# Scores of the first ten heads as one plain float32 product, and the SoLU layer beside head ten

## The chip, the cores and the metric

The kernel runs on one core of one Trainium2 chip. The metric is the device time of one execution in microseconds. TensorE is called PE in the profile, VectorE DVE, ScalarE ACT, GpSimd POOL, SyncE SP.

## The reference

Three layers are computed one after the other.

```python
# attention: 4 batches, 8 heads, 576 tokens, head size 64
scores = scale * q @ k.T
cum    = cumsum(log(clip(f, 1e-4, 1)))
scores = where(causal, -1e9, scores + cum[:, None] - cum[None, :])
attn   = softmax(scores) @ v
# SoLU layer: 2304 tokens, 512 -> 1024 -> 512
h   = x @ w_in
ln  = layernorm(h * softmax(h)) * g_ln
x   = ln @ w_out
# mixture of 8 experts, the best 2 of each token, 512 -> 1024 -> 512
logits = x @ w_gate + log1p(exp(x @ w_noise)) * noise
out    = sum over the top 2 of weight * relu(x @ w1[e]) @ w2[e]
```

All data are float32, and so is the result.

## The kernel before

**Number formats on PE.** A float32 operand is mostly split into a rounded float32r part and the float32r remainder, and a product is made of float32r products of these parts. The product of attention weights with V is plain float32 in the first `PLAIN_AV` = 13 heads, and split after them.

**One head.** Thirty-two heads are worked off in order; heads 2p and 2p+1 form a pair. `load_raw` brings queries and keys of a head, both transposed, as one tile of 128 partitions by 576. `prep` (L216) makes four operand tiles of it: QA and KB by copies on ScalarE (L223, L224), KA and QB by copies on GpSimd (L225, L226), the remainders by a subtraction on VectorE (L227, into KB) and one on GpSimd (L228, into QB). Four sets of these tiles exist, so a head uses set h % 4. Two more rows in the upper half of KA hold the head's decay (the cumulated logarithm, in two parts), and the same rows of QA hold ones, so that the decay is added by the product itself. `load_ext` loads these rows. `set_init` fills what is not loaded with zeros and ones.

`scores` (L248) computes five row blocks of 128 queries, up to the diagonal; the last block of 64 rows is shared by the two heads of a pair. Each block takes two products, QB with KB (L283) and QA with KA (L284). VectorE subtracts the mask and takes the row maximum (L286), ScalarE takes the exponential and the row sum (L288). `normalize` scales the rows on GpSimd (L301). `etrans` transposes the blocks on PE (L321), ScalarE copies them out (L325); from head 13 on VectorE also makes a remainder. `av` multiplies with V (L350 plain, L370 split) and ScalarE writes the result to XT (L354). Accumulators are three large ones (last row block, transposes, product with V) and two small ones (the other row blocks).

**Front.** `cum_prep` computes the decay of all heads on 32 partitions: clip on VectorE (L179), logarithm on ScalarE (L180), scan on VectorE (L184), two parts (L186, L187), and writes it to memory. Then heads 0 to 12 run alone. Beside each of them one or two of sixteen chunks of the SoLU weights are unpacked and split (`load_w`, L393, by `FRONT_W`): ACT, DVE four times, ACT, then GpSimd (L412) or DVE (L417), all through a single tile `wasm`.

**Middle.** After head 12, `init_dram` (L680) writes zeros to the output (18 DMAs) and fills two tables, from tiles that share buffers with the weight chunks. Then `merge` interleaves the text of the remaining heads with SoLU tiles of 128 tokens: `m_split` (L431, L432) on GpSimd, two times twelve products (L444), statistics, eight transposes (L488), 24 products (L499), gate and routing. The four batches give groups of heads 13 to 17 with tiles 0 to 3, heads 18 to 25 with tiles 4 to 8, heads 26 to 33 with tiles 9 to 12. The remaining tiles and the experts follow without attention.

**Order.** The text order is only a priority: a planner of the framework places the instructions of each engine, and each engine then works its list off in order. So the products of tile 0 (L444) run from 151 us on, beside head 12.

Of the kernel before, what the change touches and what calls it, by code (L numbers as in the profile page):

```python
# [9 lines left out]
F32 = mybir.dt.float32  # L10
F32R = mybir.dt.float32r
# [4 lines left out]
ALU = mybir.AluOpType  # L16
AX = mybir.AxisListType

MASKED = 1.0e9

PLAIN_AV = 13

TOP_OF_SMALLEST = struct.unpack("f", struct.pack("I", 896 << 20))[0]

# [2 lines left out]
def kernel(  # L27
# [18 lines left out]
    nc = tc.nc  # L46
    P = 128
# [29 lines left out]
    att = ExitStack()  # L77
    ap_ = att.enter_context(tc.tile_pool(name="att", bufs=1, side="right"))

    wpools = [wp, wp]  # L80
    turn = [0]

# [13 lines left out]
    def f32(t):  # L96
        return t.bitcast(F32)


    identf = cst.tile([P, P], F32, name="identf")  # L100
    make_identity(nc, identf)

    swapf = cst.tile([P, P], F32, name="swapf")
    for j in range(2):
        nc.vector.tensor_copy(swapf[:, j * D:(j + 1) * D], identf[:, (1 - j) * D:(2 - j) * D])

    maskr = cst.tile([P, FULL], BF, name="maskr")
    nc.vector.memset(maskr, 0.0)
    nc.gpsimd.affine_select(out=maskr[:, FULL - P:], in_=maskr[:, FULL - P:], pattern=[[-1, P]], base=0,
                            channel_multiplier=1, compare_op=ALU.is_ge, fill=-MASKED / QSC)  # L110
    maskt = cst.tile([P, S], BF, name="maskt")
    nc.vector.memset(maskt, 0.0)
    for j in range(2):
        nc.vector.tensor_copy(maskt[j * TAIL:(j + 1) * TAIL, FULL:],
                              maskr[j * TAIL:(j + 1) * TAIL, FULL - P + j * TAIL:FULL - P + (j + 1) * TAIL])
    SUMS = [cst.tile([P, NQ], F32, name=f"sums{i}") for i in range(3)]
    for t in SUMS:
        nc.vector.memset(t, 1.0)
# [4 lines left out]
    count = cst.tile([P, E], F32, name="count")  # L123
    ebase = cst.tile([P, E], F32, name="ebase")
    mhalf = cst.tile([P, 1], F32, name="mhalf")

    def routing_constants():
        nc.vector.memset(ones_b, 1.0)
# [20 lines left out]

    UP, EXT = slice(0, D), slice(D, P)  # L150
    SETS = 4
    QW = FULL + P
    QA, QB, KA, KB = ([ap_.tile([P, n], F32R, name=f"{nm}{i}") for i in range(SETS)]
                      for nm, n in (("qa", QW), ("qb", QW), ("ka", S), ("kb", S)))
# [4 lines left out]
    def set_init(i, eng):  # L159
        j = i % 2  # L160
        eng.memset(f32(KA[i])[EXT], 0.0)
        eng.memset(f32(QA[i])[EXT], 0.0)
        eng.memset(f32(QA[i])[D:D + 2, HELD[j]], 1.0)
        eng.memset(f32(QA[i])[UP, FREE[j]], 0.0)
        eng.memset(f32(QB[i])[:, FREE[j]], 0.0)

    set_init(0, nc.gpsimd)
    set_init(1, nc.vector)

    VN = [ap_.tile([P, NQ, P], F32, name=f"vn{i}") for i in range(2)]  # L170
    for t in VN:
        nc.vector.memset(t[:D, NQ - 1, :], 0.0)
    CC = []

    def cum_prep():
# [16 lines left out]

    def load_raw(h):

        if h < NH:
            RAW[h] = ap_.tile([P, S], F32, tag="raw", name=f"raw{h}", bufs=2)
            nc.sync.dma_start(RAW[h], qk[h])

    def load_ext(h):

        if h < NH:
            i = h % SETS
            if h < 2:
                for j in range(2):
                    nc.sync.dma_start(f32(KA[i])[D + j:D + j + 1, :], f32(CC[0])[h:h + 1, j, :])
            else:
                nc.sync.dma_start(f32(KA[i])[D:D + 2, :], cumd[h])

    def load_v(p):
        if p < NH // 2:  # L210
# [4 lines left out]

    def prep(h):  # L216

        if h >= NH:
            return
        i = h % SETS  # L220
        raw = RAW.pop(h)
        d = HELD[h % 2]
        nc.scalar.activation(QA[i][UP, d], raw[UP], AF.Copy)  # L223
        nc.scalar.activation(KB[i][EXT], raw[EXT], AF.Copy)  # L224
        nc.gpsimd.tensor_scalar(KA[i][UP], f32(KB[i])[EXT], 1.0, 1.0, op0=ALU.mult, op1=ALU.mult)  # L225
        nc.gpsimd.tensor_scalar(QB[i][UP, d], f32(QA[i])[UP, d], 1.0, 1.0, op0=ALU.mult, op1=ALU.mult)  # L226
# [4 lines left out]
    VS2 = []  # L231

    def vs_init():
        VS2.extend(vsp.tile([P, NQ, P], F32R, name=f"vs{i}") for i in range(2))

    def vsplit(h):
# [11 lines left out]
    def scores(h, rs):  # L248
# [11 lines left out]
        for r in rs:  # L260
# [17 lines left out]
            for a, z in cuts:  # L278
                o = ps[:, o0 + a:o0 + z]
                for j in heads:  # L280
                    i = (h // 2 * 2 + j) % SETS
                    qs = LAST[j] if tail else slice(j * P + diag, j * P + diag + P)
                    nc.tensor.matmul(o, QB[i][:, qs], KB[i][:, a:z], start=j == heads[0], stop=False)  # L283
                    nc.tensor.matmul(o, QA[i][:, qs], KA[i][:, a:z], start=False, stop=j == heads[-1])  # L284
            e = ap_.tile([P, N], F32, tag=f"e{r}", name=f"e{h}_{r}", bufs=2)
# [47 lines left out]
    def av(h):  # L333
# [38 lines left out]
        lo = vsp.tile([P, S], F32, tag="avl", name=f"avl{h}", bufs=1)[r0:r0 + D]  # L372
        nc.scalar.activation(lo, ps[D:, o0:o0 + S], AF.Copy)
        x = XT[b][r0:r0 + D, hh // 2, :]
        nc.vector.tensor_add(x, ps[:D, o0:o0 + S], lo)
# [314 lines left out]
            nc.sync.dma_start(ov[c], zt)  # L690

    def attn_stream(h):
        load_raw(h + 3)
        load_ext(h + 2)
        if h < NH:
            scores(h, (4, 3))
            yield 1200
            scores(h, (2, 1, 0))
            yield 940
            normalize(h)  # L700
        for _ in range(FRONT_W[h] if h < len(FRONT_W) else 0):
            more_w()
        prep(h + 2)
        if 0 <= h - 2 < NH:
            av(h - 2)
            yield 1700
        if h % 2 == 1:
            load_v(h // 2 + 1)
        vsplit(h)
        if 0 <= h - 1 < NH:  # L710
            etrans(h - 1, 0)
            yield 1000
            etrans(h - 1, 1)
            yield 600
# [35 lines left out]
    def run_all(g_):  # L750
        for _ in g_:
            pass
# [23 lines left out]
    def more_w():  # L776
        if wn[0] < 2 * KC + FC:
            load_w(wn[0])
            wn[0] += 1
# [2 lines left out]
    stage = stack.enter_context(tc.tile_pool(name="stage", bufs=1, side="right"))  # L782
    cum_prep()
    for h in range(2):
        load_raw(h)
    load_v(0)
    for h in range(2):
        prep(h)
        load_ext(h)
    load_raw(2)  # L790
    for i in (2, 3):
        set_init(i, nc.gpsimd)
    load_small()
    routing_constants()

    def att_part(hs):
        for h in hs:
            yield from attn_stream(h)


    FRONT_W = (1, 1, 1, 1, 1, 1, 1, 1, 1, 2, 2, 2, 1)
    run_all(att_part(range(len(FRONT_W))))
    init_dram()
    stack.close()
    vsp = att.enter_context(tc.tile_pool(name="vsp", bufs=1, side="right"))
# [151 lines left out]
```

## Time and profile before

| | |
|---|---|
| median of 3 runs | 1045.58 us (1044.43 to 1046.62) |
| profiled execution | 1044.73 us, of which the span of the profile is 1043.0 us |
| PE busy | 939.2 us, 90% of the span |
| VectorE, ScalarE, GpSimd busy | 561.0, 444.5, 469.0 us |
| mean granted clock of PE | 0.963 of full speed |

The time of the profiled execution is its span plus 1.73 us. Busy times of different engines overlap. Idle time of an engine is put down to the instruction whose end released it.

### The profile page before, as it was taken

To read this page: it belongs to the slowest core of one execution; us is meant where nothing else is said; L and a number is where in the kernel's file an instruction comes from. 1 tells how busy PE (TensorE), PEld (TensorE's weight loads), DVE (VectorE), ACT (ScalarE), POOL (GpSimd) and SP (SyncE) were. 2 spreads that over 40 slices of the span, in tenths; PEclk is the share of its full clock that TensorE was granted. 3 is DMA by queue.
4 is the path that set the end of the run, shared out by engine and by line. 5 is a ranking of instruction groups with operands and counts; after the bars stand their busy time and mean duration, and the time that the engine had idled before them with its cause. 6 is when DMAs were issued, how large, how long until landed. Compare 5 with 4: busy or idle time off the path is not lost. (4 is left out here: it accounts for less than half of the span.)

```text
span 1043.0 us, 14547 instructions
## 1 busy us (share of the span) xinstructions
PE 939.2 (90%) x5164; PEld 809.4 (78%) x5164; DVE 561.0 (54%) x1387; ACT 444.5 (43%) x831; POOL 469.0 (45%) x561
## 2 busy tenths in 40 slices
PE   3767787999999889999978999999999999999995
PEld 2545565787888778877867789898998989898994
DVE  7665877577778667756556244444443334444220
ACT  4676775556666555543343033232231323232110
POOL 7786776667767755543432223231413232230201
PEclk9988888999999999999988999999999999999998
DMA  5223336111111100031034335453434344451201
GB/s 142 85 78 107 96 107 220 63 45 35 49 42 45 46 11 22 11 92 51 23 92 112 93 117 189 141 165 122 141 112 147 102 156 149 141 168 61 78 11 38
DMA packets 55221, 96.54 MB, mean 93 GB/s; under 512 B 15398, under 2 KB 24870, under 8 KB 55144
## 3 DMA queue, kind: packets, MB, share of 16 engines
q1 hardware_dynamic: 44792, 66.41, 21.1%
q0 software_dynamic: 10352, 29.15, 8.4%
q8 instruction: 43, 0.70, 0.3%
q14 instruction: 34, 0.28, 0.1%
HBM read 76.16 MB, written 20.40 MB: 93 GB/s over the span
## 5 line engine op out<-in xcount | busy, mean ns | idle before, releaser
L649 PE MATMUL f<-fxh,we 128*128 128x256 f32 (+1 forms) x1024 | 172.3, 310 | 0.8 <-ACT fxh L632 0.8
L667 PE MATMUL f<-we,fhh 128*128 128x512 f32 x640 | 161.9, 396 | 0.0
L649 PEld LDWEIGHTS f<-fxh,we 128*128 128x128 f32 x1024 | 155.9, 189 | 1.2 <-ACT fxh L632 1.0
L667 PEld LDWEIGHTS f<-we,fhh 128*128 128x128 f32 x640 | 117.8, 188 | 24.4
L606 POOL DMA_INDIRECT row<-xdram,gi x40 | 40.2, 1005 | 211.2 <-PE fxT L629 197.3
L283 PE MATMUL s<-kb,qb 128*128 128x512 f32 (+3 forms) x192 | 73.6, 393 | 50.3 <-POOL qb L228 23.4
L654 DVE SCALAR_TENSOR_TENSOR fhl<-f,fhh 128x768 fp32r<-128x768 f32 (+1 forms) x64 | 52.7, 823 | 119.3 <-ACT fhh L653 110.8
L288 ACT ACTIVATE e<-e,nmax 128x384 f32<-128x384 f32 (+4 forms) x144 | 83.0, 577 | 60.6 <-DVE nmax L286 59.9
L301 POOL TENSOR_SCALAR e<-e,rc 128x256 f32<-128x256 f32 (+3 forms) x144 | 93.6, 667 | 31.9 <-DVE rc L298 14.3
L653 ACT ACTIVATE fhh<-f 128x768 fp32r<-128x768 f32 (+1 forms) x64 | 45.0, 704 | 139.8 <-PE f L649 129.8
L649 PE MATMUL f<-fxl,we 128*128 128x256 f32 (+1 forms) x512 | 96.3, 310 | 0.0
L283 PEld LDWEIGHTS s<-kb,qb 128*128 128x128 f32 x192 | 40.8, 214 | 70.3 <-POOL qb L228 26.8
L586 DVE TENSOR_TENSOR we<-raw,we 128x1024 fp32r<-128x1024 f32 x64 | 78.4, 1235 | 29.9 <-ACT we L585 26.8
L444 PE MATMUL m<-w_it,xh 128*128 128x512 f32 x288 | 85.2, 414 | 6.2 <-POOL xh L431 3.6
L585 ACT ACTIVATE we<-raw 128x1024 fp32r<-128x1024 f32 x64 | 66.9, 1056 | 53.5 <-PE f L667 24.7
L675 POOL DMA_INDIRECT out_dram<-y,gi x40 | 41.7, 1041 | 103.9 <-DVE y L674 79.4
L674 DVE SCALAR_TENSOR_TENSOR y<-f,tab,pv 128x512 f32<-128x512 f32 x35 | 26.3, 751 | 112.6 <-PE f L667 112.6
L667 PE MATMUL f<-we,fhl 128*128 128x512 f32 x320 | 80.4, 393 | 2.3 <-issue 2.3
L649 PEld LDWEIGHTS f<-fxl,we 128*128 128x128 f32 x512 | 80.7, 189 | 0.0
L632 ACT ACTIVATE fxh<-fxT 128x512 fp32r<-128x512 f32 x40 | 23.4, 596 | 129.5 <-PE fxT L629 129.5
L286 DVE CUSTOM_DVE_ANT_0 e<-s,maskr 128x512 f32<-128x512 f32 (+3 forms) x128 | 60.6, 485 | 32.8 <-PE s L284 26.5
L667 PEld LDWEIGHTS f<-we,fhl 128*128 128x128 f32 x320 | 60.0, 188 | 16.3 <-issue 2.7
(157 smaller groups left out, 1824.4 us busy)
## 6 DMA issues: line engine op xcount, KB each, us to landing
raw<-in_moe_w_dram SPq DMA_DIRECT2D x64, 512.0 KB
raw<-in_qk_dram SPq DMA_DIRECT2D x32, 288.0 KB
out_dram<-zt SPq DMA_DIRECT2D x18, 256.0 KB
xdram<-x SPq DMA_DIRECT2D x18, 256.0 KB
vn<-in_v_dram SPq DMA_DIRECT2D x16, 256.0 KB
wraw<-in_moe_w_in_dram SPq DMA_DIRECT2D x8, 512.0 KB
wraw<-in_moe_w_out_dram SPq DMA_DIRECT2D x8, 512.0 KB
row<-xdram,gi POOLq DMA_INDIRECT x40
```

The lines of the kernel that those rows point to most:

```text
L283: nc.tensor.matmul(o, QB[i][:, qs], KB[i][:, a:z], start=j == heads[0], stop=False)
L286: nc.vector.tensor_tensor_reduce(e, ps[:, o0:o0 + N], mask, -QSC, 3.0e38, ALU.add, ALU.min, nmax[:, r:r + 1])
L288: nc.scalar.activation(e, e, AF.Exp, bias=nmax[:, r:r + 1], scale=-1.0, accum_out=sums[:, r:r + 1])
L301: nc.gpsimd.tensor_scalar(e, e, rc[:, r:r + 1], 1.0, op0=ALU.mult, op1=ALU.mult)
L444: nc.tensor.matmul(ps, a[:, kk, :], w[:, kk, n * 512:(n + 1) * 512], start=i == 0, stop=i == 3 * KC - 1)
L585: nc.scalar.activation(hi[:, d], raw, AF.Copy)
L586: nc.vector.tensor_sub(lo[:, d], raw, f32(hi)[:, d])
L649: nc.tensor.matmul(ps[:, j], w[:, kk, (c + j) * P:(c + j + 1) * P], x[:, kk, :], start=i == 0, stop=i == 3 * KC - 1)
L653: nc.scalar.activation(hh[:, d], ps, AF.Relu)
L654: nc.vector.scalar_tensor_tensor(hl[:, d], ps, 0.0, f32(hh)[:, d], op0=ALU.max, op1=ALU.subtract)
L667: nc.tensor.matmul(ps, a[:, kk, d], w[:, kk, :], start=i == 0, stop=i == 3 * EC - 1)
L675: nc.gpsimd.indirect_dma_start(out[:, :], bass.IndirectOffsetOnAxis(ap=si[:, j:j + 1], axis=0), y, None, bounds_check=NTOK - 1, oob_is_err ...
```

## The change

For heads 0 to 9 (`PLAIN_S` = 10) queries and keys are loaded by two DMAs straight into operand tiles QP and KP, which also hold the decay rows and the ones; `prep` does nothing for them, and each row block takes one plain float32 product of QP and KP where it took two float32r ones. There are four sets of QP and KP, in a pool that is closed when head 10 begins. The split tiles are made later: sets 2 and 3 at head 5, sets 0 and 1 at head 10, in the space of the closed pool; their zeros are all written by GpSimd.

The front now ends with head 9. `init_dram` stands there, and the merge begins at head 10: its first group holds heads 10 to 17 with tiles 0 to 3. `FRONT_W` gives one weight chunk to each of heads 0 to 7 and two to each of heads 8 to 11, so that the last four chunks fall into the merge. The product with V is plain for 12 heads in place of 13. In the setup, the decay and the zeros of sets 0 and 1 come first, then the identity, the masks and other constants, then the zeros of sets 2 and 3.

```diff
-PLAIN_AV = 13
+PLAIN_AV = 12
+PLAIN_S = 10
...
+    plains = ExitStack()
+    plain = plains.enter_context(tc.tile_pool(name="plain", bufs=1, side="left"))
...
+    def attention_constants():
+        make_identity(nc, identf)
+        nc.vector.memset(maskr, 0.0)
...
+        for j in range(2):
+            nc.vector.tensor_copy(swapf[:, j * D:(j + 1) * D], identf[:, (1 - j) * D:(2 - j) * D])
+        for t in VN:
+            nc.vector.memset(t[:D, NQ - 1, :], 0.0)
...
+    QA, QB, KA, KB = ([None] * SETS for _ in range(4))
+    QP, KP = ([plain.tile([P, n], F32, name=f"{nm}{i}") for i in range(SETS)] for nm, n in (("qp", QW), ("kp", S)))
...
-    set_init(0, nc.gpsimd)
-    set_init(1, nc.vector)
+    def ext_init(q, k, j):
+        nc.gpsimd.memset(k[EXT], 0.0)
+        nc.gpsimd.memset(q[EXT], 0.0)
+        nc.gpsimd.memset(q[D:D + 2, HELD[j]], 1.0)
+        nc.gpsimd.memset(q[UP, FREE[j]], 0.0)
+
+    def set_init(i, pool):
+        for t, nm, n in ((QA, "qa", QW), (QB, "qb", QW), (KA, "ka", S), (KB, "kb", S)):
+            t[i] = pool.tile([P, n], F32R, name=f"{nm}{i}")
+        ext_init(f32(QA[i]), f32(KA[i]), i % 2)
+        nc.gpsimd.memset(f32(QB[i])[:, FREE[i % 2]], 0.0)
...
-        if h < NH:
+        if h < PLAIN_S:
+            i = h % SETS
+            nc.sync.dma_start(QP[i][UP, HELD[h % 2]], qk[h, :D])
+            nc.sync.dma_start(KP[i][UP], qk[h, D:])
+        elif h < NH:
...
-        if h >= NH:
+        if h < PLAIN_S or h >= NH:
             return
...
+                    if h < PLAIN_S:
+                        nc.tensor.matmul(o, QP[i][:, qs], KP[i][:, a:z],
+                                         start=j == heads[0], stop=j == heads[-1])
+                        continue
                     nc.tensor.matmul(o, QB[i][:, qs], KB[i][:, a:z], start=j == heads[0], stop=False)
                     nc.tensor.matmul(o, QA[i][:, qs], KA[i][:, a:z], start=False, stop=j == heads[-1])
...
     def attn_stream(h):
+        if h == PLAIN_S - 5:
+            for i in (2, 3):
+                set_init(i, ap_)
+        elif h == PLAIN_S:
+            plains.close()
+            late = att.enter_context(tc.tile_pool(name="late", bufs=1, side="left"))
+            for i in (0, 1):
+                set_init(i, late)
...
+        if h == len(FRONT_W):
+            stack.close()
+            vs_init()
...
     for h in range(2):
+        ext_init(QP[h], KP[h], h)
         load_raw(h)
+        load_ext(h)
+    attention_constants()
     load_v(0)
-    for h in range(2):
-        prep(h)
-        load_ext(h)
+    for h in (2, 3):
+        ext_init(QP[h], KP[h], h % 2)
     load_raw(2)
-    for i in (2, 3):
-        set_init(i, nc.gpsimd)
...
-    FRONT_W = (1, 1, 1, 1, 1, 1, 1, 1, 1, 2, 2, 2, 1)
-    run_all(att_part(range(len(FRONT_W))))
+    FRONT_W = (1, 1, 1, 1, 1, 1, 1, 1, 2, 2, 2, 2)
+    run_all(att_part(range(H + 2)))
     init_dram()
-    stack.close()
-    vsp = att.enter_context(tc.tile_pool(name="vsp", bufs=1, side="right"))
-    vs_init()
...
-        hs = range(max(b * H + 2, len(FRONT_W)), (b + 1) * H + 2)
+        hs = range(b * H + 2, (b + 1) * H + 2)
```

## Rows read from the trace of the kernel before

**Rows 1.** The page: busy us of each engine, share of the span, instructions; PEld is weight loads.

```profile
PE 939.2 (90%) x5164; PEld 809.4 (78%) x5164; DVE 561.0 (54%) x1387; ACT 444.5 (43%) x831; POOL 469.0 (45%) x561
```

**Rows 2.** Stretches: length, busy PE, PEld, DVE, ACT, POOL, PE clock, DMA share, GB/s.

```profile
20.00:120.00 100.00, 73.23 (x349) 53.94 (x348) 70.30 (x175) 70.06 (x154) 73.24 (x81) 0.88 0.30 90
120.00:180.00 60.00, 45.65 (x206) 35.80 (x206) 42.94 (x96) 39.82 (x80) 43.70 (x51) 0.81 0.44 150
...
240.00:360.00 120.00, 113.08 (x665) 96.81 (x664) 90.88 (x275) 76.64 (x165) 85.02 (x114) 1.00 0.15 44
...
165.00:170.00 5.00, 5.00 (x22) 4.01 (x22) 4.37 (x9) 1.20 (x3) 4.72 (x4) 0.73 0.99 377
```

**Rows 3.** PE's waits, 20 to 120 us: total, times, longest.

```profile
PE s L283 <- POOL qb L228: 9.8, 5, 2.7
...
PE s L283 <- ACT xT L354: 5.2, 3, 2.7
PE s L283 <- DVE kb L227: 2.3, 1, 2.3
```

**Rows 4.** Timeline of PE: start, us, instructions; the wait before them in brackets.

```profile
58.48 0.61 PE L283 MATMUL s<-kb,qb 128*128 128x288 f32 x1 [2.37 <-POOL qb L228]
...
59.12 0.44 PE L283 MATMUL s<-kb,qb 128*128 128x288 f32 x1
59.37 0.44 PE L284 MATMUL s<-ka,qa 128*128 128x288 f32 x1
...
131.16 1.14 PE L350 MATMUL av<-et,vn 128*128 128x128 f32 x4
...
134.14 1.81 PE L321 MATMUL eT<-identf,e 128*128 128x128 f32 x15
...
150.95 1.09 PE L444 MATMUL m<-w_it,xh 128*128 128x512 f32 x4
...
153.71 0.28 PE L283 MATMUL s<-kb,qb 128*128 128x256 f32 x1
```

**Rows 5.** Timeline of POOL: the normalization of heads 0, 10, 18 and 26.

```profile
23.92 3.27 POOL L301 TENSOR_SCALAR e<-e,rc 128x512 f32<-128x512 f32 x5 [3.20 <-DVE rc L297]
...
126.88 3.70 POOL L301 TENSOR_SCALAR e<-e,rc 128x576 f32<-128x576 f32 x5 [3.21 <-DVE rc L298]
...
248.40 3.28 POOL L301 TENSOR_SCALAR e<-e,rc 128x576 f32<-128x576 f32 x5
...
370.35 3.37 POOL L301 TENSOR_SCALAR e<-e,rc 128x576 f32<-128x576 f32 x5 [3.90 <-DVE rc L298]
```

**Rows 6.** Groups by line, 20 to 120 us: busy us, mean ns, idle before.

```profile
L228 POOL TENSOR_TENSOR qb<-raw,qa 64x576 fp32r<-64x576 f32 x10 | 15.0, 1498 | 0.8
...
L227 DVE TENSOR_TENSOR kb<-raw,kb 64x576 fp32r<-64x576 f32 x10 | 13.6, 1358 | 0.7 <-issue 0.2 <-ACT kb L224 0.2
...
L226 POOL TENSOR_SCALAR qb<-qa 64x576 fp32r<-64x576 f32 x10 | 9.8, 980 | 11.3 <-ACT qa L223 9.4 <-DVE rc L298 1.7
...
L225 POOL TENSOR_SCALAR ka<-kb 64x576 fp32r<-64x576 f32 x9 | 6.8, 759 | 0.8
L224 ACT ACTIVATE kb<-raw 64x576 fp32r<-64x576 f32 x10 | 6.8, 681 | 0.2
```

**Rows 7.** Timeline of the setup, all engines.

```profile
1.07 0.58 POOL L161 MEMSET ka<- 64x576 f32 x1
...
6.11 0.68 ACT L180 ACTIVATE ftlf<-ftlf 32x576 f32<-32x576 f32 x1
...
7.54 1.80 DVE L184 TENSOR_TENSOR_SCAN cs<-ftlf 32x576 f32<-32x576 f32 x1
...
9.37 1.78 DVE L227 TENSOR_TENSOR kb<-raw,kb 64x576 fp32r<-64x576 f32 x1
...
15.22 0.58 PE L284 MATMUL s<-ka,qa 128*128 128x288 f32 x1 [3.27 <-DMA ka<-cc]
```

**Rows 8.** Timeline of SP's queue: the first nine zero writes.

```profile
162.90 5.16 SPq L690 DMA_DIRECT2D out_dram<-zt  x9
```

More of the change, by code (lines that the diff above doesn't have):

```diff
@@ L100 @@
     identf = cst.tile([P, P], F32, name="identf")
-    make_identity(nc, identf)
     swapf = cst.tile([P, P], F32, name="swapf")
-    for j in range(2):
-        nc.vector.tensor_copy(swapf[:, j * D:(j + 1) * D], identf[:, (1 - j) * D:(2 - j) * D])
     maskr = cst.tile([P, FULL], BF, name="maskr")
-    nc.vector.memset(maskr, 0.0)
-    nc.gpsimd.affine_select(out=maskr[:, FULL - P:], in_=maskr[:, FULL - P:], pattern=[[-1, P]], base=0,
-                            channel_multiplier=1, compare_op=ALU.is_ge, fill=-MASKED / QSC)
     maskt = cst.tile([P, S], BF, name="maskt")
[L112 to L115, printed above, removed]
     SUMS = [cst.tile([P, NQ], F32, name=f"sums{i}") for i in range(3)]
-    for t in SUMS:
-        nc.vector.memset(t, 1.0)
     ones_b = cst.tile([P, P], BF, name="ones_b")
@@ L125 @@
     mhalf = cst.tile([P, 1], F32, name="mhalf")
+    def attention_constants():
+        make_identity(nc, identf)
+        nc.vector.memset(maskr, 0.0)
+        nc.gpsimd.affine_select(out=maskr[:, FULL - P:], in_=maskr[:, FULL - P:], pattern=[[-1, P]], base=0,
+                                channel_multiplier=1, compare_op=ALU.is_ge, fill=-MASKED / QSC)
+        nc.vector.memset(maskt, 0.0)
+        for j in range(2):
+            nc.vector.tensor_copy(maskt[j * TAIL:(j + 1) * TAIL, FULL:],
+                                  maskr[j * TAIL:(j + 1) * TAIL, FULL - P + j * TAIL:FULL - P + (j + 1) * TAIL])
+        for t in SUMS:
+            nc.vector.memset(t, 1.0)
+        for j in range(2):
+            nc.vector.tensor_copy(swapf[:, j * D:(j + 1) * D], identf[:, (1 - j) * D:(2 - j) * D])
+        for t in VN:
+            nc.vector.memset(t[:D, NQ - 1, :], 0.0)
     def routing_constants():
@@ L151 @@
     SETS = 4
+    assert PLAIN_S % SETS == 2
     QW = FULL + P
-    QA, QB, KA, KB = ([ap_.tile([P, n], F32R, name=f"{nm}{i}") for i in range(SETS)]
-                      for nm, n in (("qa", QW), ("qb", QW), ("ka", S), ("kb", S)))
+    QA, QB, KA, KB = ([None] * SETS for _ in range(4))
+    QP, KP = ([plain.tile([P, n], F32, name=f"{nm}{i}") for i in range(SETS)] for nm, n in (("qp", QW), ("kp", S)))
     LAST = (slice(FULL, QW), slice(0, P))
@@ L157 @@
     FREE = (slice(S, QW), slice(0, QW - S))
[L159 to L165, printed above, removed]
-    set_init(0, nc.gpsimd)
-    set_init(1, nc.vector)
+    def ext_init(q, k, j):
[8 more added lines that the diff above has]
+        nc.gpsimd.memset(f32(QB[i])[:, FREE[i % 2]], 0.0)
     VN = [ap_.tile([P, NQ, P], F32, name=f"vn{i}") for i in range(2)]
-    for t in VN:
-        nc.vector.memset(t[:D, NQ - 1, :], 0.0)
     CC = []
@@ L202, in load_ext @@
             i = h % SETS
+            t = KP[i] if h < PLAIN_S else f32(KA[i])
             if h < 2:
                 for j in range(2):
-                    nc.sync.dma_start(f32(KA[i])[D + j:D + j + 1, :], f32(CC[0])[h:h + 1, j, :])
+                    nc.sync.dma_start(t[D + j:D + j + 1, :], f32(CC[0])[h:h + 1, j, :])
             else:
-                nc.sync.dma_start(f32(KA[i])[D:D + 2, :], cumd[h])
+                nc.sync.dma_start(t[D:D + 2, :], cumd[h])
     def load_v(p):
@@ L231 @@
     VS2 = []
+    VSP = []
     def vs_init():
+        vsp = att.enter_context(tc.tile_pool(name="vsp", bufs=1, side="right"))
+        VSP.append(vsp)
         VS2.extend(vsp.tile([P, NQ, P], F32R, name=f"vs{i}") for i in range(2))
@@ L371, in av @@
         r0 = (hh % 2) * D
-        lo = vsp.tile([P, S], F32, tag="avl", name=f"avl{h}", bufs=1)[r0:r0 + D]
+        lo = VSP[0].tile([P, S], F32, tag="avl", name=f"avl{h}", bufs=1)[r0:r0 + D]
         nc.scalar.activation(lo, ps[D:, o0:o0 + S], AF.Copy)
```

## The prediction

> **What bounds the kernel now.** I read the page first, then busy time by stretch, then the waits of TensorE (PE), then the timelines of single engines.
>
> The span is 1043.0 us, and PE is busy for 90% of it [rows 1]; what lies around the span is 1.73 us (1044.73 us in all). So PE is the bound on average, and the question is where it is not. The table by stretch answers that [rows 2]. From 20 to 120 us, the front, where attention heads run alone, PE is busy for 73.2 of 100 us at a granted clock of 0.88, and VectorE, ScalarE and GpSimd are each busy for 70 to 73: nobody is full. From 120 to 180 us the picture is the same with a lower clock, 0.81. From 240 us on, where SoLU tiles run beside heads, PE is busy for 113.1 of 120 us at 1.00. The room is therefore in the first 180 us, and after that PE sets the pace. Every change of work on PE counts there; work on the other three engines hardly does.
>
> The speed of the front is read from the GpSimd timeline: the normalization of a head (L301) marks heads evenly. Head 0 starts it at 23.92 us, head 10 at 126.88, head 18 at 248.40, head 26 at 370.35 [rows 5]. That is 103.0 us for ten heads, 10.30 us each, then 121.5 us for eight heads with four SoLU tiles, then 122.0 us for eight heads with five tiles.
>
> Why a front head takes 10.30 us though no engine has more than 7.6 us of work in it: PE's waits [rows 3]. Of 26.8 us idle in the 100 us, 9.8 end with the last split of the queries on GpSimd (L228) and 2.3 with that of the keys on VectorE (L227): 12.1 us are the preparation of the split operands. Another 5.2 end with ScalarE freeing the accumulator of the product with V (L354). A wait costs twice: after 2.37 us of it the products of 288 columns start 0.24 us apart [rows 4], 1.2 columns a ns, which is the 1.2 GHz level; at 2.4 GHz it would be half of that.
>
> **Part by part.** *Scores of heads 0 to 9.* Two float32r products for each row block become one float32 product. A head has 128+256+384+512 columns in its four full row blocks and 576 as its share of the last one, which a pair shares: 1856 columns, 3712 column-passes when split. Price of a float32r column: twelve products of 512 columns take 150.95 to 153.71 us [rows 4], 0.449 ns a column. Price of a plain float32 column: the product with V of the first heads is already plain. From 131.16 to the next transposes at 134.14 us lie its 1600 columns and two split products of 128 columns (0.11 us) [rows 4]: 2.87 us, 1.79 ns a column, four times as much. So scores go from 3712 x 0.449 = 1.67 us to 1856 x 1.79 = 3.32 us: 1.66 us more PE work a head at full clock, 16.6 us for the ten, twice that at the low level. This is the price of the change.
>
> *Preparation of heads 0 to 9 goes.* Ten heads cost GpSimd 15.0 + 9.8 + 6.8 us (one of L225's ten falls outside the window), VectorE 13.6 and ScalarE two copies of 6.8 each [rows 6]: 3.2, 1.4 and 1.4 us a head. None of these engines is full, so by itself this is worth nothing; its worth is the 12.1 us of PE waits, and part of the 5.2 us, because the two copies stand ahead of that eviction on ScalarE. The queries and keys now land straight in the operand tiles, three heads ahead, so nothing on an engine stands between the load and the product.
>
> *Pace of a front head after.* PE's work now: 73.23 us over 100/10.30 = 9.7 heads, 7.54 us, which is 6.64 at full clock (x 0.88). After: 6.64 + 1.66 = 8.30. Lower bound: PE runs as in 240 to 360 us, 94% busy at clock 1.00: 8.8 us. Upper bound: clock stays at 0.88 and only the 12.1 us go: 8.30/0.88 + 14.7/9.7 = 10.9 us. I take 9.6, a little on the good side of the middle, because the other three engines get emptier (GpSimd from 7.5 to 4.3 us a head) and each wait that goes takes half-speed products with it. Ten heads then gain 10 x 0.7 = 7 us (bounds +15 and -6).
>
> The Trainium skill speaks against the clock rising: "TensorE: Matmul & The Clock Gate", Part 4, says that transposes do not count as activity for the clock. A front head has fifteen of them. By that rule the clock would stay at 0.88 and the head near 10.9 us, the total unchanged. The trace does not bear it out: the stretch 240 to 360 us has the same transposes in it and is granted 1.00 [rows 2].
>
> *Setup.* Now the decay rows are late: the logarithm (ScalarE, 6.11 us) stands behind two preparation copies, the scan ends at 9.34, then VectorE splits the second head's keys from 9.37 to 11.15 before it can finish the rows, and PE's first complete product starts at 15.22, on their DMA [rows 7]. Without the preparation the logarithm can start about 1.4 us sooner and the last step another 1.8 us sooner. The new zero-fills on GpSimd, four for each of four sets (about 0.6 us for a large one [rows 7]), and the constants after them, now in that order, take some 9 us and lie under this chain, as the routing constants do; if not, each set costs about 2 us. About 3 us earlier, of which the first two heads, with four-fold products on a possibly slow clock, give some back: at 1.2 GHz their scores cost up to 6.6 us more, of which the waits of that stretch hide most. I take 2.5 us, bounds 0 and 5.
>
> *SoLU beside head ten.* Heads 10, 11, 12 and tiles 0 to 3 are already between 126.88 and 248.40 us, so the work of that stretch is not changed, only its mixture: the merge begins at head 10 in place of head 13. Best case by the next stretch: 122.0 us for eight heads and five tiles [rows 5]. A tile is 48 products of 512 columns (11.0 us) and some 1.5 us of transposes, with its gate about 13.3 us; 108.7 us without it, and 111.6 with the heads whose product with V is plain (2 x 1.43). That would be 10 us less than 121.5. Against it stands the start of the SoLU chain, whose first tile waits in turn for VectorE, ScalarE and GpSimd, and the last four weight chunks, which are now split beside tiles. I take 4 us.
>
> *The rest.* The zero-fills of sets 2 and 3 at head 5 and of 0 and 1 at head 10 are ten memsets each, some 4 us on GpSimd, under the 3.2 us a head that it is relieved of; uncovered, 8 us. Each plain head issues two half-size loads in place of one on SP's queue, prefetched three heads ahead. Head 12's product with V becomes split: PE 2.87 to 1.44 us, for two GpSimd and two VectorE passes of 1 to 2 us each, which lie under PE; 1 us, left in the rounding.
>
> **Sum.** 2.5 + 7 + 4 = 13.5 us: 1044.7 - 13.5 = 1031.2 for the profiled execution. The median shown is 0.85 us above it, so 1032.
>
> **Rivals.** *PE fills up (0.22).* The front reaches 8.8 us a head and the middle stretch its 10 us: 15 + 2.5 + 10 = 27.5 us, 1018. For it: the busy 94% later on. Against it: the front has one chain per head and few accumulators, and nothing else for PE to do. The Trainium skill's "Perfetto Trace Analysis", § Identifying the Most-Contended Engine, would side with this rival: it judges PE by weight-load busy time, which is 53.9 us here [rows 2], and by it the added 1.66 us vanish in slack. I don't go by it, since the columns alone make over 6 us a head.
>
> *Clock and remaining waits stay (0.08).* 10.9 us a head takes 6 us back, and the sum is about zero: 1045.
>
> *The front becomes slower (0.14).* One mechanism: PE's idle time does not shrink, because the waits for L228 are only the last of several and the next comes as late: the score's maximum on VectorE, which is still interleaved with weight chunks, or the decay rows. Then 8.30/0.88 + 2.76 = 12.2 us a head, 19 us more, less 6.5: 1058. It decides from 11.2 us a head on.
>
> *Zero writes in the way (0.08).* The zeros for the output, 18 DMAs on SP, and two table fills now precede the last four weight chunks and the loads of heads 13 and on, and share the chunks' buffers. Before they came last. Nine of them (2.36 MB), issued in one go [rows 8], keep the DMA engines 99% busy at 377 GB/s [rows 2], 6.3 us: some 13 us for all. If ScalarE, in order, waits for a chunk behind them, the middle stretch loses 9 to 13 us in place of gaining 4: 1045 to 1049. Against it: heads 10 to 12 and the first products of three tiles are ready meanwhile.
>
> **Chances and range.** Forecast 0.48 (1023 to 1041). About 2.1 us, 0.2%, is what a measurement of this kernel can tell from no change. Faster 0.78: the forecast, the full PE, and half of the two cases around zero. Same 0.07. Slower 0.15. The range 1013 to 1047 leaves out most of the slower rival and the best of the full PE.
>
> **What would show it.** Right: no GpSimd, VectorE or ScalarE preparation before head 10; head 0's normalization near 21 us, head 10's near 117, head 18's near 235; PE's granted clock in the front near 0.95, its idle time below 1.5 us a head; plain score products in pairs of records like those of L350. Wrong: a pace above 10.3 us a head; PE waits that end with DVE nmax or a DMA in the place of L228; a hole in PE after head 10 that ends with ScalarE's L404 or a weight chunk; anything behind 250 us other than a shift.

## The result, and the profile after

The changed kernel takes 1032.6 us (median of four runs, 1029.38 to 1033.38), the kernel before 1046.1 us beside it (1044.43 to 1046.88). The ratio is 0.9867, 95% interval [0.9842, 0.9892]. The forecast was 1032. The total came out right by luck: the terms for the setup and the front together were 18 us too small, and the term for the early start of the layer had the wrong sign and was off by 18 us the other way.

The page of the changed kernel: PE has 5.8 us more work than in [rows 1], VectorE 16.3 less, ScalarE 12.8, GpSimd 28.4.

```profile
span 1031.6 us, 14508 instructions
...
PE 945.0 (92%) x5164; PEld 808.1 (78%) x5164; DVE 544.7 (53%) x1375; ACT 431.7 (42%) x811; POOL 440.6 (43%) x554
```

Busy time by stretch, columns as in [rows 2]:

```profile
20.00:120.00 100.00, 84.40 (x394) 60.33 (x394) 61.88 (x170) 67.02 (x149) 61.03 (x85) 0.91 0.46 147
120.00:180.00 60.00, 53.68 (x279) 41.95 (x278) 45.85 (x119) 41.14 (x86) 36.63 (x45) 0.97 0.31 100
180.00:240.00 60.00, 48.97 (x265) 41.18 (x264) 40.83 (x101) 32.48 (x71) 40.28 (x56) 0.89 0.13 36
240.00:360.00 120.00, 111.71 (x639) 95.22 (x638) 85.53 (x273) 72.71 (x157) 79.74 (x105) 0.97 0.13 41
```

The first two stretches are fuller. The third is new: from 180 to 240 us PE is busy for only 49.0 of 60 us at 0.89, where before it was 57.2 at 0.99:

```profile
180.00:240.00 60.00, 57.24 (x327) 48.58 (x326) 38.04 (x126) 35.49 (x79) 37.40 (x51) 0.99 0.19 57
```

The changed kernel wins early and gives a part back behind 180 us.

GpSimd's timeline gives the marks that answer to [rows 5], the normalization (now L324) of heads 0, 10, 18 and 26:

```profile
18.17 2.77 POOL L324 TENSOR_SCALAR e<-e,rc 128x512 f32<-128x512 f32 x5 [3.77 <-DVE rc L320]
...
114.43 2.77 POOL L324 TENSOR_SCALAR e<-e,rc 128x576 f32<-128x576 f32 x5 [0.76 <-DVE rc L321]
...
236.41 3.28 POOL L324 TENSOR_SCALAR e<-e,rc 128x576 f32<-128x576 f32 x5 [0.43 <-DVE rc L321]
...
359.64 3.37 POOL L324 TENSOR_SCALAR e<-e,rc 128x576 f32<-128x576 f32 x5 [4.10 <-DVE rc L321]
```

Head 0 is 5.8 us earlier, ten front heads take 96.3 us (9.63 each) in place of 103.0, the next eight heads with four tiles 122.0 in place of 121.5, and what follows head 18 795.2 in place of 794.6. Read that way, the gain is 5.8 + 6.7 and nothing behind head 10. The experiments show that this reading is misleading: two large terms cancel there.

PE's waits from 20 to 120 us (engine, line, releaser, total, times, longest), against [rows 3]:

```profile
PE s L303 <- DVE nmax L309: 4.3, 5, 1.4
PE m L467 <- POOL xh L454: 3.7, 1, 3.7
PE s L303 <- ACT xT L377: 3.6, 1, 3.6
PE av L373 <- ACT et L348: 2.6, 2, 1.5
```

The 12.1 us of waits for the preparation are gone, and 15.6 us of idle time stay: the score's maximum on VectorE, ScalarE's evictions, and the first tile's input.

### The profile page after: what moved, and what is told of

Its sections match the earlier page's. It is cut to its first block, busy times and chain, and to the rows that moved or that the text cites. A ratio compares the mean times of both kernels' runs of the same rounds, so it can differ in the third digit from the quotient of the medians.

```text
span 1031.6 us, 14508 instructions
## 1 busy us (share of the span) xinstructions
PE 945.0 (92%) x5164; PEld 808.1 (78%) x5164; DVE 544.7 (53%) x1375; ACT 431.7 (42%) x811; POOL 440.6 (43%) x554
## 5 line engine op out<-in xcount | busy, mean ns | idle before, releaser
L311 ACT ACTIVATE e<-e,nmax 128x256 f32<-128x256 f32 (+3 forms) x144 | 83.0, 578 | 61.1 <-DVE nmax L309 60.9
L324 POOL TENSOR_SCALAR e<-e,rc 128x256 f32<-128x256 f32 (+3 forms) x144 | 88.7, 632 | 39.2 <-DVE rc L321 20.3
L467 PE MATMUL m<-w_it,xh 128*128 128x512 f32 x288 | 92.1, 436 | 11.8 <-POOL xh L454 9.1
L522 PE MATMUL m<-w_ot,lh 128*128 128x512 f32 x288 | 73.9, 397 | 3.4 <-ACT w_ot L439 3.3
L467 PEld LDWEIGHTS m<-w_it,xh 128*128 128x128 f32 x288 | 57.1, 208 | 23.2 <-POOL xh L454 12.8
```

The costliest lines, as they stand in the source:

```text
L311: nc.scalar.activation(e, e, AF.Exp, bias=nmax[:, r:r + 1], scale=-1.0, accum_out=sums[:, r:r + 1])
L324: nc.gpsimd.tensor_scalar(e, e, rc[:, r:r + 1], 1.0, op0=ALU.mult, op1=ALU.mult)
L467: nc.tensor.matmul(ps, a[:, kk, :], w[:, kk, n * 512:(n + 1) * 512], start=i == 0, stop=i == 3 * KC - 1)
L522: nc.tensor.matmul(ps, a[:, kk, :], w[:, kk, :], start=i == 0, stop=i == 3 * FC - 1)
```

## The experiments

The diff has three separable parts: the order of the setup, the plain scores, and the layer's start at head ten. Six of the eight combinations ran, the two kernels among them (plain scores were not tried with the old setup). Medians in us; the kernel before took between 1046.1 and 1047.05 beside them, and single runs of one kernel lie up to 12 us apart:

| setup | scores | layer beside head 13 | layer beside head 10 | the early start costs |
|---|---|---|---|---|
| old | split | 1046.5 (before) | 1057.2 | 10.7 |
| new | split | 1031.6 | 1042.6 | 11.0 |
| new | plain | 1018.8 | 1032.6 (changed) | 13.8 |

Down a column, the setup brings 14.9 and 14.6 us while the scores are split, and the plain scores bring 12.8 and 10.0 with the new setup. From before to the changed kernel: -14.9 - 12.8 + 13.8 = -13.9. The first two shares hold for this order of adding the parts. Both parts take away PE's waits for the preparation, so the plain scores may be worth more, and the setup less, where they are added the other way round. What the table gives without that choice is their sum: 27.7 us (1046.5 to 1018.8).

**Plain scores and the new setup, without the early start.**

```diff
-PLAIN_AV = 12
+PLAIN_AV = 13
-    FRONT_W = (1, 1, 1, 1, 1, 1, 1, 1, 2, 2, 2, 2)
-    run_all(att_part(range(H + 2)))
+    FRONT_W = (1, 1, 1, 1, 1, 1, 1, 1, 1, 2, 2, 2, 1)
+    run_all(att_part(range(len(FRONT_W))))
...
-        hs = range(b * H + 2, (b + 1) * H + 2)
+        hs = range(max(b * H + 2, len(FRONT_W)), (b + 1) * H + 2)
```

> Plain scores of heads 0 to 9 and the new setup, but the merge begins at head 13 as before, with the old weight-chunk schedule and place of the zero writes. If the gain is made in setup and front (theory A: after's marks give 5.8 us up to head 0's normalization and 6.7 us from there to head 10's), this kernel keeps it: 12 us faster than before, about 1034 us. If the gain comes from beginning the SoLU layer beside head ten (theory B), it is within 3 us of before, about 1045 us.

Measured: 1018.78 us (1014.17 to 1021.25), 0.9725 [0.9694, 0.9755], 13.8 us better than the whole change, and better than either theory expected. From head 0's mark to head 10's, and from there to head 18's (columns as in [rows 2]):

```profile
19.05:112.47 93.42, 79.52 (x392) 56.02 (x391) 67.95 (x185) 71.17 (x161) 58.63 (x77) 0.98 0.43 132
112.47:221.43 108.96, 99.43 (x531) 83.25 (x530) 75.75 (x204) 69.29 (x146) 77.70 (x102) 0.93 0.30 99
```

Against the kernel before, head 0 is 4.9 us earlier, the ten front heads take 9.5 us less, and the next eight 12.5 us less.

**The early start alone**, in the kernel before: the same lines the other way, with the closing of the weights' pool moved to where the last chunk is split.

```diff
-PLAIN_AV = 13
+PLAIN_AV = 12
...
+        if h == len(FRONT_W):
+            stack.close()
+            vs_init()
...
-    FRONT_W = (1, 1, 1, 1, 1, 1, 1, 1, 1, 2, 2, 2, 1)
-    run_all(att_part(range(len(FRONT_W))))
+    FRONT_W = (1, 1, 1, 1, 1, 1, 1, 1, 2, 2, 2, 2)
+    run_all(att_part(range(H + 2)))
...
-        hs = range(max(b * H + 2, len(FRONT_W)), (b + 1) * H + 2)
+        hs = range(b * H + 2, (b + 1) * H + 2)
```

> Split scores and setup as before, but the merge begins at head 10, with the new weight-chunk schedule, place of the zero writes and 12 plain products with V. Theory A: nothing is won there, within 3 us of before, about 1046 us (in the changed kernel the stretch from head 10's to head 18's normalization took 122.0 us against 121.5). Theory B: 8 us or more faster, 1038 us or less.

Measured: 1057.2 us (1052.42 to 1060.57), 1.0102 [1.0069, 1.0134]. The forecast gave this part a gain of 4; it loses 10.7, which neither theory had foreseen. Two of PE's waits from head 10's mark (130.51 us) to head 18's (259.48) are long here:

```profile
PE m L447 <- POOL xh L434: 11.7, 2, 6.3
PE m L502 <- ACT w_ot L419: 6.0, 3, 4.4
```

In the kernel before, the same stretch has 3.6 us of the first kind and none of the second.

**The order of the setup alone**, scores split, layer beside head thirteen:

```diff
-    set_init(0, nc.gpsimd)
-    set_init(1, nc.vector)
...
     for h in range(2):
+        set_init(h, nc.gpsimd)
         load_raw(h)
+        load_ext(h)
+    attention_constants()
...
         prep(h)
-        load_ext(h)
```

> The kernel before with its setup in the changed order: decay first, then zeros of the first two sets on GpSimd, loads, decay rows, constants, and only then the preparation of heads 0 and 1. If the order makes the start earlier (theory S), head 0's normalization comes 4 to 6 us sooner and the time falls by 4 to 6 us. If it is the missing preparation (theory A), the split operands are as late as the decay was: 0 to 2 us, 1044 to 1046 us.

Measured: 1031.64 us (1029.1 to 1034.22), 0.9858 [0.9829, 0.9886]. This was the surprise, well outside both theories: an order of instructions, with the same work (the zeros of one set move from VectorE to GpSimd), is worth as much as the whole change. Its marks are 19.1, 113.4 and 233.9 us: head 0 is 4.8 us earlier, and the ten front heads take 94.3 us with their preparation still in place. What differs is read from GpSimd's timeline of this kernel:

```profile
19.09 0.69 POOL L301 TENSOR_SCALAR e<-e,rc 128x512 f32<-128x512 f32 x1
...
21.10 0.67 POOL L225 TENSOR_SCALAR ka<-kb 64x576 fp32r<-64x576 f32 x1
21.85 1.06 POOL L226 TENSOR_SCALAR qb<-qa 64x576 fp32r<-64x576 f32 x1
22.90 0.57 POOL L301 TENSOR_SCALAR e<-e,rc 128x384 f32<-128x384 f32 x1
23.55 1.40 POOL L228 TENSOR_TENSOR qb<-raw,qa 64x576 fp32r<-64x576 f32 x1
25.06 1.54 POOL L301 TENSOR_SCALAR e<-e,rc 128x576 f32<-128x576 f32 x3
26.57 0.83 POOL L226 TENSOR_SCALAR qb<-qa 64x576 fp32r<-64x576 f32 x1
27.48 1.46 POOL L228 TENSOR_TENSOR qb<-raw,qa 64x576 fp32r<-64x576 f32 x1
```

The preparation of heads 2 and 3 stands between the row blocks of head 0's normalization, and head 3's last split (L228) starts at 27.48 us. In the kernel before, GpSimd normalizes all of head 0 first (23.92 us, [rows 5]), and head 3's split starts at 36.20:

```profile
36.20 1.39 POOL L228 TENSOR_TENSOR qb<-raw,qa 64x576 fp32r<-64x576 f32 x1
```

The lead of 8.7 us is not used up: the later splits stay ahead of PE. From 20 to 112 us PE waits for L228 once, for 0.4 us, in place of the 9.8 us of [rows 3], and 4.3 us are left of all its waits for the preparation:

```profile
PE s L284 <- POOL ka L225: 2.1, 1, 2.1
PE s L283 <- DVE kb L227: 1.8, 4, 1.0
PE s L283 <- POOL qb L228: 0.4, 1, 0.4
```

In two other kernels below with this setup and split scores, head 0's mark is at 21.0 and 21.1 us and head 3's split at 29.4 and 29.5, so head 0 is 2.8 to 4.8 us earlier and the lead is 6.7 to 8.7 us. No run moved the preparation of these two heads alone: that the lead sets the pace of the front is read from the traces, not shown by itself. Busy time of that stretch, first in the kernel with the new order alone:

```profile
20.00:112.00 92.00, 73.24 (x383) 54.88 (x382) 71.20 (x183) 74.28 (x163) 78.81 (x87) 0.96 0.33 104
```

and in the kernel before:

```profile
20.00:112.00 92.00, 67.82 (x317) 49.82 (x316) 62.70 (x162) 64.17 (x142) 66.71 (x75) 0.87 0.28 84
```

GpSimd does more in the same time, PE does more, and the granted clock is 0.96 in place of 0.87.

**No preparation for heads 4 to 9**, in the kernel before. Their queries and keys are neither loaded nor split, and their scores are made from the operands of heads 0 to 3.

```diff
-        if h < NH:
+        if h < NH and not 4 <= h < 10:
...
-        if h >= NH:
+        if h >= NH or 4 <= h < 10:
             return
```

> The kernel before, in which heads 4 to 9 are neither loaded nor prepared: their split products read the operands of heads 0 to 3, so the scores of six heads are not theirs. It shows what the preparation costs without the price of plain products. Theory A: the waits for it are 1.25 us a head, and the half-speed products after them some 0.8 us more, so 2 us a head, 12 us, about 1034 us. Rival (the next wait takes the place of L228's): less than 0.6 us a head, 1042 us or more.

Measured: 1015.19 us (1010.25 to 1019.67), 0.97 [0.9667, 0.9733]. Six heads' preparation, with its loads, costs 31 us in the old order, so the forecast's reading that the preparation holds the front was right. It is worth over twice the 12 us expected from PE's waits for it: in this trace the ten front heads take 81.6 us in place of 103.0, and the next eight 112.4 in place of 121.5. What the forecast missed as well is that placing the preparation earlier can hide much of it.

**Plain scores made twice**, in the version without the early start: each plain product is issued two times.

```diff
-            for a, z in cuts:
+            for a, z in [c for c in cuts for _ in range(2 if h < PLAIN_S else 1)]:
```

> The kernel plain_scores_only with every plain score product of heads 0 to 9 issued twice, the second overwriting the first: 3.32 us more of PE a head by the price in the prediction, 33 us in all. If PE sets the pace of the front, 33 us more than 1018.8, 1052 us. If the 14 us that PE idles there take up a part, 19 to 26 us more, 1038 to 1045 us. If the front is set by something else, under 10 us.

Measured: 1046.98 us (1045.5 to 1053.99), 28.2 more than without. PE's busy time rises by 30.1 us (971.8 against 941.7), 3.0 a head where the forecast had 3.32. So some nine tenths of work that is added to PE in the front lengthens the program. In the traces the ten front heads take 124.3 us in place of 93.4, with 27.8 us more of PE's work, and PE's idle time there grows from 13.9 to 16.9 us:

```profile
21.28:145.54 124.26, 107.33 (x497) 75.86 (x496) 78.72 (x211) 78.75 (x170) 62.44 (x82) 0.96 0.45 142
```

The added products stand on PE and also in each head's chain from scores to product with V. The run does not tell which of the two makes them count.

**The zeros of the output later**, in the changed kernel, behind the second merged group:

```diff
-        zt = stage.tile([P, DM], F32, tag="wraw", name="zt", bufs=2)
+    def zero_out():
+        zt = ap_.tile([P, DM], F32, tag="e3", name="zt", bufs=2)
...
+        if b == 2:
+            zero_out()
```

> The changed kernel with the 18 zero writes of the output put after the second merged group; the two table fills stay. Beginning the SoLU layer at head ten cost 14 us (1032.6 against 1018.8 us for plain scores alone). Theory Z (the zero writes stand on SP ahead of weight chunks and operand loads): this gives back 6 to 13 us, 1020 to 1026 us. Theories W and M: within 3 us of the changed kernel, 1030 to 1035 us.

Measured: 1030.85 us (1028.77 to 1033.69), no difference that can be told from 1032.6. The 18 writes do not cost the 6 to 13 us of theory Z.

**All weight chunks before head ten**, in the changed kernel:

```diff
-    FRONT_W = (1, 1, 1, 1, 1, 1, 1, 1, 2, 2, 2, 2)
+    FRONT_W = (1, 1, 1, 1, 2, 2, 2, 2, 2, 2)
```

> The changed kernel with all sixteen weight chunks at heads 0 to 9 (two each from head 4 on) and none in the merge. Theory W (the last chunks are split beside tiles, and PE waits 3.3 us for them in the product with w_out): 3 to 10 us faster than the changed kernel, 1022 to 1029 us. Theories Z and M: 1031 to 1036 us, the front a little slower because VectorE has more to do in it.

Measured: 1032.97 us (1032.72 to 1034.71), no difference; the ten front heads take 96.3 us in both traces. The last four chunks inside the merge are not what costs either, at this mixture.

**Another mixture**, in the changed kernel: the merge counts a head of the first group as 7000 in place of 5440, so that fewer steps of the layer stand before each head.

```diff
-        merge(att_part(hs), 5440.0 * len(hs), chain(moe_stream(t, t1) for t in range(t0, t1)), 12660.0 * (t1 - t0))
+        merge(att_part(hs), (7000.0 if b == 1 else 5440.0) * len(hs), chain(moe_stream(t, t1) for t in range(t0, t1)), 12660.0 * (t1 - t0))
```

> The changed kernel with heads favoured in the first merged group (7000 in place of 5440 for a head). In the changed kernel tile 3 is through at 200 us, heads 15 to 17 then run alone, and PE waits 5.3 us for the split of tile 4, which needs head 15. Theory M (the mixture is at fault): 4 to 10 us faster, 1022 to 1028 us. Theories Z and W: 1030 to 1035 us.

Measured: 1024.68 us (1022.36 to 1029.51), 0.9807 [0.9778, 0.9836], 7.9 us better than the changed kernel. The step that it repairs is seen in PE's timeline of the changed kernel:

```profile
226.87 2.08 PE L467 MATMUL m<-w_it,xh 128*128 128x512 f32 x4 [5.34 <-POOL xh L454]
228.74 1.91 PE L467 MATMUL m<-w_it,xl 128*128 128x512 f32 x4
...
238.05 1.09 PE L467 MATMUL m<-w_it,xl 128*128 128x512 f32 x4
```

and in GpSimd's, just before:

```profile
218.85 1.41 POOL L244 TENSOR_TENSOR qb<-raw,qa 64x576 fp32r<-64x576 f32 x1
...
222.47 1.40 POOL L244 TENSOR_TENSOR qb<-raw,qa 64x576 fp32r<-64x576 f32 x1
223.98 2.47 POOL L324 TENSOR_SCALAR e<-e,rc 128x512 f32<-128x512 f32 x4
226.41 0.40 POOL L454 TENSOR_SCALAR xh<-xT 128x256 fp32r<-128x256 f32 x1
```

The layer has run ahead of the heads: a tile's products wait for `xh`, a copy of 0.40 us on GpSimd, which stands behind two splits and a whole normalization. The last part of its input, written for head 15, was there by 219.8 us:

```profile
219.05 0.75 DVE L398 TENSOR_TENSOR xT<-av,avl 64x576 f32<-64x576 f32 x1
```

After the wait four of PE's products of 512 columns take 2.08 us, the next four 1.91, and four of the same form 1.09 at 238.05 us. With 7000 no such wait in the stretch reaches 1 us. But then it is VectorE's score maximum that ends the most idle time there, against 2.6 us in the changed kernel and 1.3 us in the best one below:

```profile
PE s L306 <- DVE nmax L309: 8.0, 4, 3.6
```

The last four combine these parts. **The change without plain scores** (new setup and early start, split scores): the diff of the early start on top of that of the setup, and `prep` for every head.

```diff
-                    if h < PLAIN_S:
-                        nc.tensor.matmul(o, QP[i][:, qs], KP[i][:, a:z],
-                                         start=j == heads[0], stop=j == heads[-1])
-                        continue
                     nc.tensor.matmul(o, QB[i][:, qs], KB[i][:, a:z], start=j == heads[0], stop=False)
```

> The changed kernel with the ten heads' scores as split products again: the new order of the setup and the early start of the layer stay. Theory A (the plain product is worth its 12.9 us also here, as it was with the layer at head thirteen): 1031.6 for the setup alone plus 11 to 14 for the early start, 1042 to 1046 us. Theory B (the plain product's gain came from the stretch behind head thirteen, and with the early start only its price of some 14 us is left): 1018 to 1030 us. Within 2 us of the changed kernel's 1032.6: gain and price cancel here.

Measured: 1042.6 us (1038.71 to 1050.39), 0.9964 [0.9943, 0.9984]. Theory A holds: in the change, too, plain scores bring 10 us.

**The new setup with 7000**, split scores, layer beside head thirteen; the line of the mixture above on top of the setup's diff:

```diff
+        merge(att_part(hs), (7000.0 if b == 1 else 5440.0) * len(hs), ...
```

> Only the changed setup order, split scores, the layer beside head thirteen, and each head of the first merged group costed at 7000 instead of 5440, so that fewer of the layer's steps are put before a head. If the 12 us that plain scores gain behind head thirteen are only the mixture of heads and layer: 1020 to 1025 us. If they come from preparation that the split subtractions hold back on GpSimd: 1029 to 1033 us, no change from the setup order alone (1031.6).

Measured: 1026.31 us (1024.69 to 1034.25), 0.9816 [0.9785, 0.9848]. It lies between the two theories' ranges: 5.3 us come from the mixture, though two of its six runs (1032.1 and 1034.3) lie among those without it. They are not the plain scores' gain, because the next kernel still has that.

**Plain scores, the new setup and 7000**, layer beside head thirteen: the same line in the version without the early start.

```diff
+        merge(att_part(hs), (7000.0 if b == 1 else 5440.0) * len(hs), ...
```

> Plain scores and the new setup order, the layer beside head thirteen, and the heads of the first merged group costed at 7000. If heads ahead of the layer are good wherever the layer starts: 1011 to 1017 us against 1018.8 without it. If the cost only repaired what the start at head ten had spoilt: 1016 to 1022 us, no change.

Measured: 1014.14 us (1012.24 to 1019.86), 0.9694 [0.967, 0.9718]. This is the best time of all: 18.5 us below the changed kernel and 32.9 below the one before. Against the kernel before it, plain scores are worth 12.2 us at this mixture too. The mixture's own 4.6 us are less sure, since the single runs of the two kernels overlap.

**The change with 9000:**

```diff
-        merge(att_part(hs), 5440.0 * len(hs), ...
+        merge(att_part(hs), (9000.0 if b == 1 else 5440.0) * len(hs), ...
```

> The changed kernel with the first merged group's heads costed at 9000 (7000 gave 1024.7, 5440 gives 1032.6). If the loss of the early start is the layer's share before each head, more of the same cost gives more: 1017 to 1022 us, as with the layer at head thirteen. If 7000 has already taken the waits for the fourth tile's input away and the rest is another cause: 1023 to 1028 us.

Measured: 1028.97 us (1024.45 to 1030.54), 0.9818 [0.9796, 0.984]: no better than 7000, by the median 4.3 us worse, and just above the second range expected. PE now waits 5.2 us for a weight chunk (`w_ot`, once 4.8 us) between heads 10 and 18. More of the same is not better.

Busy time from head 10's mark to head 18's shows what is still open. First the changed kernel, then the changed kernel with 7000:

```profile
114.43:236.41 121.98, 104.62 (x554) 84.77 (x552) 84.63 (x214) 73.52 (x154) 77.63 (x100) 0.93 0.26 83
```

```profile
114.37:226.28 111.91, 96.87 (x547) 79.74 (x545) 86.43 (x213) 71.78 (x152) 76.48 (x98) 0.98 0.29 90
```

and the best kernel, with the layer beside head thirteen:

```profile
111.90:215.73 103.83, 96.30 (x525) 80.05 (x523) 75.08 (x203) 68.16 (x144) 75.93 (x99) 0.96 0.32 104
```

With 7000 PE has nearly the same work as in the best kernel, and 15.0 us idle in place of 7.5. VectorE has 11.3 us more to do there. The weight chunks are not the reason: each of the two stretches holds four of them on VectorE, 18.4 us of work with 7000 and 17.0 in the best kernel.

## Why the prediction came out right, and which of its steps did not

*What bounds the kernel.* Right in the main. The front was idle for its preparation (31 us for six heads without it), and work added to PE there counts (28.2 us for 30.1 us of added products), as far as that run can tell PE from the heads' chain.

*Price of the plain product.* Both prices were too low, that of the split products by more, so the difference came out too large. The records of ten heads' score products keep PE busy for 34.7 us split, with the new setup (first row; busy time stands behind the comma), and for 40.6 us plain, in the kernel without the early start (second row). That is 3.5 and 4.1 us a head, where the forecast had 1.67 and 3.32:

```profile
5.00:100.00 95.00, 34.72 (x120) 0.96 0.36 108
5.00:130.00 125.00, 40.58 (x120) 23.37 (x120) 0.95 0.41 121
...
240.00:362.00 122.00, 20.62 (x99) 1.00 0.15 44
```

The third row is the kernel before at full clock: 99 split products, some eight heads, at 2.5 us a head. The split price was read from the layer's products of 512 columns in a row, at full clock. In the changed kernel split products of 288 columns start 0.13 us apart from 220.2 us on, 0.45 ns a column too, but each is recorded with 0.29 us; so a short group takes more time a column by its last record. And a part of the front's products ran at the low level, as in [rows 4]. The exchange adds 6.0 us to PE's busy time with the layer at head thirteen (935.7 to 941.7), 1.3 at the other mixture (936.8 to 938.1) and 1.9 with the early start (943.1 to 945.0), not 16.6. These differences are rough: the mixture alone moves that time by 9.3 us at the same work (945.0 to 935.7 with 7000).

*Preparation and pace of the front, 7 us.* The mechanism is right, and the size was low: plain scores bring 10.0 to 12.8 us on top of the new setup, which has itself taken most of the preparation's waits away. The place is not only the front. With the layer beside head thirteen the ten heads shrink from 94.3 to 93.4 us, and it is the middle stretch that falls, from 120.5 to 109.0 us. In the front, plain scores pay their price there; in the middle, GpSimd is further ahead of its work when the layer starts. With the early start the gain lies elsewhere: head 0 is 2.9 us earlier, the front takes 5.1 us less and the middle 3.0. PE's timeline in the middle, with the new setup alone:

```profile
162.68 1.97 PE L488 MATMUL uT<-identf,mu 128*128 128x128 f32 x8 [5.60 <-POOL mu L478]
```

and with plain scores:

```profile
149.96 1.09 PE L511 MATMUL uT<-identf,mu 128*128 128x128 f32 x8 [0.31 <-POOL mu L501]
```

In that stretch PE's waits that end with GpSimd are 12.4 us with split scores and 4.5 with plain ones; the pair with 7000 has 7.9 and 4.1, the pair with the early start 12.5 and 6.7. That is part of the 10 to 13 us in each pair; the rest was not separated.

*The clock.* It rose where PE waited less: from 20 to 112 us the kernel before was granted 0.87, the kernel with the new order alone 0.96, both with fifteen transposes a head. The Trainium skill, "TensorE: Matmul & The Clock Gate", Part 4, says that the full clock does not engage for transposes. The trace does not test that: other products stand between the transposes here, and in the stretch that the prediction set against the rule. What fails is only what the prediction drew from it, a clock that stays at 0.88. How full PE is on average does not fix the clock either. The changed kernel was granted 0.89 from 180 to 240 us, 82% busy and with the wait of 5.34 us in it; the new order alone had 0.96 from 20 to 112 us, 80% busy.

*Setup, 2.5 us.* In the changed kernel the logarithm runs at 4.19 us in place of 6.11, and PE's first product starts at 10.95, where the first complete one was at 15.22 [rows 7]; head 0 is 5.8 us earlier, and 4.5 to 5.6 in the other kernels with plain scores (not counting the doubled ones). That is at or above the bound of 5. The larger part was not priced at all: with split scores, the setup's order also decides where the preparation of heads 2 and 3 stands in GpSimd's list, and the part is worth 14.6 to 14.9 us. The text treated the setup as ending with head 0.

That lead of the preparation cannot be at work in the changed kernel, which has no preparation for these heads. There the setup can give head 0's earlier start, and the plain scores take away the same waits that the lead does. So the step that failed is best named for both terms together: the forecast had 2.5 + 7 = 9.5 us, and the runs show 27.7. The worth of the preparation was set at the 12.1 us of waits that end with it and a part of 5.2 more, and the price of the plain products at 16.6; without preparation six heads alone gave 31 us, and the products added 1.3 to 6.0 us of PE's time.

*SoLU beside head ten, +4 us.* The wrong sign: it costs 10.7 to 13.8 us. The best case had been taken from the stretch of heads 18 to 25, in which the chain of tiles was long under way; its 111.6 us is no limit either, since the middle stretch took 109.0 and 103.8 us with the layer beside head thirteen. Of the two costs named against it, the weight chunks and the start of the layer's chain, the chunks are refuted at this mixture. One contribution is seen in the traces: the layer's steps get ahead of the heads whose rows they need, and a small copy on GpSimd then stands behind a normalization. From head 10's mark to head 18's, PE's waits for that copy grow with the early start in all three pairs, from 3.6 to 11.7, 2.7 to 10.0 and 0.3 to 5.3 us. A mixture with the heads ahead gives 7.9 us back; but the same mixture gives 4.6 and 5.3 us beside head thirteen, so most of that may be a general gain. With it in both, the early start still costs 10.5 us (1024.68 against 1014.14), as PE's idle time with VectorE fuller. What makes the rest stays open: head twelve's split product with V, the mixture of eight heads in place of five, and the place of the weight chunks at this mixture were not tried.

*The rivals.* The zero writes are refuted at the size named, since moving them changes nothing that can be told. PE filling up did not come about in the changed kernel (9.63 us a head, 122.0 us in the middle); the versions without the early start come near the time that it gave, 1018, by another way. The clock and the remaining waits did not stay (0.91, and 9.63 us a head in place of 10.9). The slower front did not come. Of the waits that it named, VectorE's maximum is the largest left in the front, with 4.3 us. The idea in the Trainium skill's "Perfetto Trace Analysis", § Identifying the Most-Contended Engine, that PE is to be judged by its weight loads, would have put added products into slack, as the prediction reads it. The doubled scores speak against that reading here: weight loads were busy for 56.0 of 93.4 us in the front, and 28 of 30 us came through.

*The marks named ahead.* Head 0 at 18.2 (forecast near 21), head 10 at 114.4 (near 117), head 18 at 236.4 (near 235); the clock 0.91 (near 0.95); idle time 1.5 us a head (below 1.5). Marks of one kernel could not tell the parts from each other, since the change put all three into the same stretches.

## What to carry to other kernels

When a change has parts, price and run each part alone: here a gain of some 28 us and a loss of 14 added up to the forecast of three small gains. Where two parts may remove the same waits, their single worths hang on which is added first, so run them in both orders. A reordering of the setup is not over when the first unit of work begins, where engines follow a fixed list: look at which later preparation it puts ahead of which other work on the same engine, because here a lead of 7 to 9 us was still there ten heads later. And before a second kind of work is mixed in earlier, check that its inputs are finished by then, and which small instruction will stand behind a large one in an ordered queue.

## What the runs showed that was not expected

- Another order of the setup's instructions moved the granted clock of the front from 0.87 to 0.96, and PE got 5.4 us more busy time into 92 us.
- Plain float32 scores take 4.1 us of PE a head (a second set of the same products adds 3.0), and the split ones 3.5, or 2.5 at full clock. So the exchange adds only 1.3 to 6.0 us of busy time for ten heads: the split score products, in short groups, cost far more than 0.449 ns a column.
- Eighteen DMAs that write the zeros of the output, put before the middle stretch or far behind it, made no measurable difference (1032.6 and 1030.85 us).
